# One software DMA ring in order of use, 512 B first loads and single score groups at the head of an attention and feed-forward kernel

## The chip, the cores and the metric

The kernel runs on one core of a Trainium2 chip. The metric is the device time of one execution in microseconds (us), and every time quoted as "of runs" is a median of several executions. Beside it there are profiled executions; their span is the time from the first to the last recorded instruction, and it is 1.7 to 1.9 us shorter than the device time of the same execution.

Ratios are computed as the mean time of one kernel's fast runs over that of the kernel before's fast runs of the same rounds on the same chip, so a ratio is not quite the quotient of the medians that stand beside it.

## The reference

Attention over 4 batches, 8 heads, 768 positions and head size 64, in which retrieval heads see all earlier positions and the other heads see 4 sink positions and a window of 64; then a feed-forward layer on the 3072 tokens. Condensed from the reference:

```python
rel = pos[:, None] - pos[None, :]
causal = rel >= 0
stream_keep = causal & (is_sink | ((rel >= 0) & (rel < window)))
mask = np.where(retr[0, :, 0, 0, None, None], causal, stream_keep)
a = softmax(np.where(mask, scale * q @ k.T, -1e9))
x = (a @ v).transpose(0, 2, 1, 3).reshape(3072, 512)
h = x @ w_in                       # 512 x 2048
out = (h - np.tanh(h)) @ w_out     # 2048 x 512
```

## The kernel before

Tokens are worked in 12 tiles of 256, three to a batch. For a tile, q and k are cast to fp16 and transposed by TensorE (PE), scores are built per pair of heads (a unit, four to a tile), ACT takes the exponential, PE multiplies by v, and the result `x` is transposed and goes through `w_in` (matmuls `ph`, here called hidden units) and `w_out` (`po`, output groups). A list scheduler in Python fixes the order of each engine when the kernel is built. Each operation names its engine, an estimated length, what it reads and writes, and, for a load, its number of DMA packets. Only reads and writes of the same buffer become semaphores; an operation that is merely told to be ordered after another in the plan gets no wait on the chip.

Tiles 0 and 1 come in fp32 through the Sync engine's (SP's) DMA ring, in halves of four heads and blocks of 128 tokens:

```python
for i in blocks:
    s0 = g * TT + i * 128
    op("SP", ...,
        lambda ...: nc.sync.dma_start(
            out=raw_of(nm, t)[:, i, h0 : h0 + nh, :],
            in_=src[b, h0 : h0 + nh, s0 : s0 + 128, :].rearrange("h p d -> p h d")),
        w=[...], dma=(128 * nh, 18.3), after=after)      # 256 B rows
```

ACT, DVE and GpSimd (POOL) cast them. The weights and tile 2 come through GpSimd's own ("software") DMA ring, which casts fp32 to fp16 in flight; issuing such a load keeps GpSimd itself for 0.54 to 1.1 us in the traces. The head of the program (its first 35 us, until PE is full) is laid out like this, cut with `...`:

```python
cast_qk(0, (("ACT", "ACT"), ("ACT", "DVE")), (0,))
load(1, halves=range(2))                    # tile 1 by SP, fp32
for n in (0, 1):
    st_T(n, "ACT", "DVE")                   # transposes of unit n
    for f in scores(n): f()
...
for half in range(2):
    cast_qk(1, (("ACT", "ACT"), ("ACT", "ACT")), (half,))
    cast_v(1, ("POOL", "POOL"), (half,))
for c0, n in W_IN:
    load_w_in(c0, n, [("v1", 0, 1, 0)])     # 4 loads
for j in range(4):
    load_w_out(j, [("v1", 0, 1, 0)])        # 4 loads
load_cast(2)                                # tile 2: 6 loads, last on the ring
scale_v(0, "POOL")                          # vf = v * flag of the head
scale_v(1)
# tile 3 and on: SP loads, held by a tiny "gate" DMA that reads tile 2's k
```

The masks are DVE work: for each head `m = (A < thr) * -60000`, 128 x 512 in fp16, and for tiles 0 and 1 PE adds them to the scores through an identity matmul. A second set of eight, `A >= thr`, replaces them while tile 1 is worked; from tile 2 on DVE multiplies the exponentials by it. `scale_v` is GpSimd work, two multiplications of about 1.06 us for a tile.

The softmax here doesn't subtract the row's maximum and nothing guards it: scores larger than these inputs give would overflow.

## Time and profile before

| | before |
|---|---|
| device time, median of 3 | 242.54 us (242.09 to 242.56) |
| the profiled execution | 240.8 us, span 239.1 |
| PE busy | 221.2 of 239.1 us |
| next: ACT, DVE | 144.8, 138.3 us |

The prediction below reads the head of the profile. The columns are the stretch and its length, then the busy time of PE, of PE's weight loads, of DVE, ACT and GpSimd with their numbers of instructions, the granted clock, the DMA share and GB/s.

```profile
core 0: us, PE busy (x) PEld busy (x) DVE busy (x) ACT busy (x) POOL busy (x), PEclk, DMA share, GB/s
2.25:4.00 1.75, 0.00 (x0) 0.00 (x0) 0.33 (x2) 0.57 (x2) 0.90 (x4) 1.00 0.87 192
...
60.00:65.00 5.00, 4.26 (x67) 2.52 (x63) 2.25 (x7) 3.73 (x5) 4.69 (x12) 1.00 1.02 274
...
80.00:85.00 5.00, 4.08 (x47) 3.13 (x47) 3.42 (x12) 2.08 (x4) 2.26 (x8) 1.00 1.16 206
```

In a stretch of 5.00 us, PE was idle for 0.74 and 0.92 us, although the head was long over. And between 2.25 and 4 us the loads already moved 192 GB/s.

### The profile page before, as it was taken

Reading aid. Unit: us, or ns where it says so; the run is one execution under the profiler, and the core shown is the slowest. Engines: PE = TensorE matmul, PEld = TensorE weight load, DVE = VectorE, ACT = ScalarE, POOL = GpSimd, SP = SyncE. Lnnn points to the kernel's source line nnn. Section 1 sums busy time; section 2 is a strip of 40 time slices with the busy share of each in tenths; the row PEclk is TensorE's granted clock in tenths of the full one; section 3 lists DMA queues with packets and bytes.
Section 4 is the critical chain, followed back from the end, with each engine's and each line's share of the span. In section 5 each row is a group of like instructions: output and inputs, shape, how many; then the busy total and the mean of one; then the engine's idle time right before and its main releaser. Section 6 shows DMA issues by size and latency. Waiting matters only on the chain. (4 is left out here: it accounts for less than half of the span.)

```text
span 239.1 us, 5924 instructions
## 1 busy us (share of the span) xinstructions
PE 221.2 (93%) x2220; PEld 158.0 (66%) x2220; DVE 138.3 (58%) x343; ACT 144.8 (61%) x225; POOL 87.6 (37%) x214
## 2 busy tenths in 40 slices
PE   0877899999889899999999999999999999999992
PEld 0445678765578577777767686777777777777661
DVE  3564455584588767766765744667676537434310
ACT  3588665787658658655576738456768473443320
POOL 5286342009984558191461943724500000000000
PEclk9999999999999999999999999999999999999999
DMA  6999999997999999949989486998611111211121
GB/s 133 220 193 204 213 212 169 210 210 149 261 213 221 182 174 173 246 80 218 259 147 236 106 188 167 167 212 193 123 54 62 31 44 48 71 28 35 44 88 51
DMA packets 110338, 36.08 MB, mean 151 GB/s; under 512 B 104546, under 2 KB 106850, under 8 KB 110306
## 3 DMA queue, kind: packets, MB, share of 16 engines
q1 hardware_dynamic: 101090, 30.55, 62.3%
q0 software_dynamic: 8928, 4.98, 15.1%
q8 instruction: 18, 0.29, 0.5%
q10 hardware_dynamic: 288, 0.14, 0.2%
q14 instruction: 14, 0.11, 0.2%
HBM read 27.27 MB, written 6.29 MB: 140 GB/s over the span
## 5 line engine op out<-in xcount | busy, mean ns | idle before, releaser
L1080 PE MATMUL ph<-xT,win 128*128 128x256 f16 x768 | 101.0, 273 | 1.6 <-DMA xT<-x16t 0.9
L1139 PE MATMUL po<-wout,gt 128*128 128x512 f16 (+1 forms) x400 | 98.5, 371 | 0.2
L1093 ACT ACTIVATE th<-ph 128x512 f32<-128x512 f32 x96 | 57.3, 601 | 62.9 <-PE ph L1080 61.4
L1100 DVE SCALAR_TENSOR_TENSOR gt<-th,ph 128x512 f16<-128x512 f32 x96 | 65.3, 685 | 45.9 <-ACT th L1093 45.5
L1080 PEld LDWEIGHTS <-win 128*128 128x128 f16 x768 | 80.0, 114 | 14.1 <-issue 3.0
L906 ACT ACTIVATE pt<-sc 128x1024 f16<-128x1024 f32 (+1 forms) x78 | 68.2, 925 | 9.3 <-PE sc L886 8.1
L1139 PEld LDWEIGHTS <-gt 128*128 128x128 f16 x400 | 36.2, 98 | 25.1 <-issue 1.3
L630 POOL CAST t<-raw_rqk 128x256 f16 x72 | 27.7, 427 | 58.8 <-DMA raw_rqk<-in_k_dram 42.6
L975 PEld LDWEIGHTS <-pt 128*128 128x128 f16 x552 | 25.9, 98 | 9.9 <-issue 0.9
L975 PE MATMUL av<-v,pt 128*128 128x65 f16 x304 | 26.2, 196 | 0.3 <-ACT xT L774 0.3
L625 POOL CAST v<-raw_rv 128x128 f16 x72 | 22.5, 353 | 6.1 <-DMA raw_rv<-in_v_dram 6.1
L886 PE MATMUL sc<-qk 64*128 64x128 f16 (+1 forms) x412 | 23.0, 239 | 1.5 <-DVE qk L776 1.2
L886 PEld LDWEIGHTS <-qk 64*128 64x128 f16 x412 | 13.7, 95 | 12.6 <-issue 8.9
L1005 DVE TENSOR_TENSOR x16t<-av,rinv 128x128 f32 x72 | 20.8, 289 | 1.9
L975 PE MATMUL av<-vf,pt 128*128 128x65 f16 x248 | 19.8, 193 | 0.1
L1115 ACT ACTIVATE ot<-po 128x512 f32<-128x512 f32 (+1 forms) x24 | 14.3, 596 | 8.7 <-PE po L1139 8.7
L995 DVE RECIPROCAL rinv<-av 128x4 f32<-128x4 f32 x48 | 8.6, 179 | 17.2 <-PE av L975 17.2
L941 DVE TENSOR_TENSOR pt<-pt,m 128x1024 f16<-128x1024 f16 x16 | 11.6, 725 | 7.4 <-ACT pt L906 7.4
L931 DVE TENSOR_TENSOR pt<-pt,mS 128x512 f16<-128x512 f16 x24 | 11.1, 503 | 6.6 <-ACT pt L906 6.6
L793 PEld LDWEIGHTS <-t 128*128 128x128 f16 x48 | 4.2, 109 | 9.2 <-ACT t L594 5.7
L701 POOL TENSOR_TENSOR vf<-v,rflagr 128x260 f16<-128x260 f16 x12 | 7.3, 615 | 0.0
L471 DVE TENSOR_SCALAR m<-A,thr 128x512 f16<-128x512 f16 x16 | 5.9, 418 | 2.0 <-PE sc L873 1.6
(95 smaller groups left out, 88.7 us busy)
## 6 DMA issues: line engine op xcount, KB each, us to landing
out_dram<-ot SPq DMA_DIRECT2D x23, 256.0 KB, 2.5
raw_rqk<-in_q_dram SPq DMA_DIRECT2D x18, 256.0 KB, 4.3
raw_rqk<-in_k_dram SPq DMA_DIRECT2D x18, 256.0 KB, 4.4
raw_rv<-in_v_dram SPq DMA_DIRECT2D x18, 256.0 KB, 4.6
win<-in_moe_w_in_dram POOLq DMA_DIRECT2D x4, 512.0 KB, 9.0
wout<-in_moe_w_out_dram POOLq DMA_DIRECT2D x4, 512.0 KB, 15.9
raw_rqk<-in_q_dram SPq DMA_DIRECT2D x8, 128.0 KB, 3.8
raw_rqk<-in_k_dram SPq DMA_DIRECT2D x8, 128.0 KB, 3.8
```

The lines of the kernel that those rows point to most:

```text
L625: nc.gpsimd.tensor_copy(out=v1s[b]()[:, lo : lo + NB, rank : rank + 1, 0:D], in_=raw_of("v", t)[:, :, at, :],)
L630: nc.gpsimd.tensor_copy(out=t16[t % 2][:, :, :, rank : rank + 1, :], in_=raws["rqk", t][0]()[:, :, :, at, :],)
L886: nc.tensor.matmul(out=sc()[:, hh, o : o + nb * 128].rearrange("p (i c) -> p i c", c=128), lhsT=ks.rearrange("p i c -> p (i c)")[p_, jb * ...
L906: lambda pt=pt, gi=gi, wid=wid, sc=sc: nc.scalar.activation(out=pt()[:, :, 512 * gi : 512 * gi + wid], in_=sc()[:, :, 0:wid], func=AF.Exp, ...
L941: nc.vector.tensor_mul(out=pv, in0=pv, in1=m4[:, h0 : h0 + 2, 256:512].unsqueeze(2).to_broadcast([128, 2, 2, 256]),)
L975: nc.tensor.matmul(out=av()[:, i, hh, :], lhsT=pt()[:, hh, co : co + 128], rhs=vv, start=(jb == first_jb), stop=(jb == qb),)
L1005: nc.vector.tensor_mul(out=x16s[t]()[:, :, at, :], in0=av()[:, :, hh : hh + 1, 0:D], in1=rinv()[:, :, hh : hh + 1].unsqueeze(3).to_broadca ...
L1080: nc.tensor.matmul(out=ph()[:, j, :], lhsT=w()[:, cb, c0 + fb % 4 : c0 + 512 : 4], rhs=xTs[t]()[:, cb, :], start=(cb == 0), stop=(cb == HP ...
L1093: lambda: nc.scalar.activation(out=th()[:], in_=ph()[:], func=AF.Tanh, scale=1.0 / XS),
L1100: lambda: nc.vector.scalar_tensor_tensor(out=gts[t]()[:, u * FU : (u + 1) * FU, :], in0=th()[:], scalar=-XS, in1=ph()[:], op0=ALU.mult, op ...
L1115: nc.scalar.activation(out=ot()[:, c0:c1], in_=po()[:, c0:c1], func=AF.Copy, scale=1.0 / XS)
L1139: nc.tensor.matmul(out=po()[:, c0:c1], lhsT=gts[t]()[:, f, ts * 128 : ts * 128 + 128], rhs=w_out_t[f // 4]()[:, f % 4, c0:c1], start=(f == ...
```

## The change

The intent: what PE needs first is to land first. Tile 1 moves to the software ring, so its casts fall away; that ring is forced into one fixed order (new argument `behind`), with tile 1 and the first `w_in` chunk first, and with tile 2 between the `w_out` chunks and no longer behind them; q, k of tile 0 come in packets of two tokens (512 B); the scores of tile 1 are issued one group at a time; the eight masks of the first units are split in pairs around the key copies. The diff is shortened; `...` and `w=[...]` stand for what is left out.

```diff
-    def op(self, eng, ns, fn, r=(), w=(), dma=None, prio=None, port=False, after=None):
+    def op(self, eng, ns, fn, r=(), w=(), dma=None, prio=None, port=False, after=None, behind=None):
 ...
+        def paired(nm, t):
+            return nm != "v" and t == 0
 ...
+                    if paired(nm, t):
+                        op("SP", max(420, 128 * nh * 1.1),
+                            lambda ...: nc.sync.dma_start(
+                                out=raw_pairs(nm, t)[:, h0 : h0 + nh, :, :].rearrange(
+                                    "p h e d -> p h (e d)"),
+                                in_=src[b, h0 : h0 + nh, g * TT : (g + 1) * TT, :].rearrange(
+                                    "h (p e) d -> p h (e d)", e=NB)),
+                            w=[...], dma=(128 * nh, 26.0), after=after)
+                        continue
 ...
+                    if paired(nm, t):      # PSUM -> qk, back to the order of the tokens
+                        o = o.rearrange("p b (c e) -> p b e c", e=NB)
+                        src = src.rearrange("p e (b c) -> p b e c", b=NB)
 ...
-            two = 1 if todo[0][0] // HP in (0,) else 2
+            two = 1 if todo[0][0] // HP in (0, 1) else 2
 ...
-        load(1, halves=range(2))
+        load_cast(1, [("rv", 0, "v", 0, 1)], "qk")
+            load_w_in(*W_IN[0], ())
+            load_cast(1, (), "v")
         for n in (0, 1):
+            masks(thr, "thr", range(2 * n, 2 * n + 2), added=True)
             st_T(n, "ACT", "DVE")
 ...
-        for half in range(2):
-            cast_qk(1, (("ACT", "ACT"), ("ACT", "ACT")), (half,))
-            cast_v(1, ("POOL", "POOL"), (half,))
-            for c0, n in W_IN:
-                load_w_in(c0, n, [("v1", 0, 1, 0)])
-            for j in range(4):
-                load_w_out(j, [("v1", 0, 1, 0)])
-            load_cast(2)
-        scale_v(0, "POOL")
+            load_w_in(*W_IN[1], ())
+            load_w_in(*W_IN[2], ())
+            scale_v(0, "POOL")
+            load_w_in(*W_IN[3], ())
+            load_w_out(0, ())
+            load_cast(2, (), "q")
+            load_cast(2, (), "k")
+            load_w_out(1, ())
+            load_cast(2, (), "v")
+            load_w_out(2, ())
+            load_w_out(3, ())
         scale_v(1)
```

More of the change, by code (lines that the diff above doesn't have):

```diff
@@ L55, in op @@
         port = port or (eng == "POOL" and not dma)
-        self.ops.append((eng, ns, fn, deps, dma, i if prio is None else prio, port))
+        self.ops.append((eng, ns, fn, deps, dma, i if prio is None else prio, port, behind))
         return i
@@ L61, in run @@
         users = [[] for _ in range(n)]
+        followers = [[] for _ in range(n)]
         left = [0] * n
         for i, o in enumerate(self.ops):
-            left[i] = len(o[3])
+            left[i] = len(o[3]) + (o[7] is not None)
             for d in o[3]:
                 users[d].append(i)
+            if o[7] is not None:
+                followers[o[7]].append(i)
         ready = [0.0] * n
@@ L130, in run @@
             queue[e].remove(i)
-            _, ns, _, _, dma, _, port = self.ops[i]
+            _, ns, _, _, dma, _, port, _ = self.ops[i]
             self.start[i] = t
@@ L136, in run @@
                 self.port = free[e]
+            for u in followers[i]:
+                ready[u] = max(ready[u], t + ns)
+                left[u] -= 1
+                if not left[u]:
+                    enqueue(u)
             if dma:
@@ L293, in load @@
                         )
+                    if paired(nm, t):
+                        op(
+                            "SP", max(420, 128 * nh * 1.1),
+                            lambda nm=nm, src=src, h0=h0, nh=nh: nc.sync.dma_start(
+                                out=raw_pairs(nm, t)[:, h0 : h0 + nh, :, :].rearrange(
+                                    "p h e d -> p h (e d)"
+                                ),
+                                in_=src[b, h0 : h0 + nh, g * TT : (g + 1) * TT, :].rearrange(
+                                    "h (p e) d -> p h (e d)", e=NB
+                                ),
+                            ),
+                            w=[
+                                key for x in (range(2) if half is None else (half,))
+                                for key in raw_keys(nm, t, x)
+                            ],
+                            dma=(128 * nh, 26.0), after=after,
+                        )
+                        continue
                     for i in blocks:
@@ L307, in load, with raw_pairs @@
                         )
+        def raw_pairs(nm, t):
+            r = raws["rqk", t][0]()
+            return r[:].rearrange("p i x h d -> p (i x h d)").rearrange(
+                "p (x h e d) -> p x h e d", x=2, h=H, e=NB
+            )[:, "qk".index(nm), :, :, :]
         def raw_of(nm, t):
+            if paired(nm, t):
+                return raw_pairs(nm, t).rearrange("p h e d -> p e h d")
             r = raws["rv" if nm == "v" else "rqk", t][0]()
@@ L319, in program, with behind, load_cast, fn @@
         W_IN = ((0, 512), (512, 512), (1024, 512), (1536, 512))
-        def load_cast(t):
+        last = [None]
+        def behind(ns, fn, **kw):
+            last[0] = op("POOL", ns, fn, behind=last[0], **kw)
+        def load_cast(t, w_after=(), names="qkv"):
             b, g = divmod(t, NG)
-            for nm, src in (("q", q), ("k", k), ("v", v)):
-                def fn(nm=nm, src=src):
-                    for i in range(NB):
+            for nm in names:
+                src = {"q": q, "k": k, "v": v}[nm]
+                def fn(blocks, nm=nm, src=src):
+                    for i in blocks:
                         s0 = g * TT + i * 128
@@ L334, in fn @@
                         )
-                keys = [
-                    key for half in range(2) for key in (
-                        [("v1", b, g, half)] if nm == "v" else t16_keys(nm, t, half)
-                    )
-                ]
-                op(
-                    "POOL", 2600, fn, r=[("v1", b, 1, 0)], w=keys, dma=(2 * 128 * H, 18.5),
-                )
+                if nm == "v":
+                    for i in range(NB):
+                        behind(
+                            930, lambda fn=fn, i=i: fn((i,)), r=w_after,
+                            w=[("v1", b, g, half) for half in range(2)] if i else [("v1a", t)],
+                            dma=(128 * H, 18.5),
+                        )
+                    continue
+                for i in range(NB):
+                    behind(
+                        930, lambda fn=fn, i=i: fn((i,)), r=w_after,
+                        w=[key for half in range(2) for key in t16_keys(nm, t, half, (i,))],
+                        dma=(128 * H, 18.5),
+                    )
         def load_w_in(c0, n, w_after):
             w = lazy(w_pool, [128, HP, n], FP16, f"win{c0}", f"win{c0}")
-            op(
-                "POOL", 900,
+            behind(
+                800,
                 lambda: nc.gpsimd.dma_start(
@@ L360, in load_w_out @@
             w = lazy(w_pool, [128, 4, DM], FP16, f"wout{j}", f"wout{j}")
-            op(
-                "POOL", 900,
+            behind(
+                600,
                 lambda: nc.gpsimd.dma_start(
@@ L462, in masks @@
         def masks(threshold, key, heads, added=False):
-            for h in range(heads):
+            for h in heads:
                 how = (
@@ L476, in masks @@
                 )
-        masks(thr, "thr", H, added=True)
         RANK = [4 * (hp % 2) + 2 * (hp // 2) + hh for hp in range(HP) for hh in range(2)]
@@ L596, in cast_op, with t16_keys @@
                 op(e, cost, lambda: engs[e].tensor_copy(out=dst(), in_=src()), r=r, w=w, port=True)
-        def t16_keys(nm, t, half):
-            return [("t16", t % 2, nm, half)]
+        def t16_keys(nm, t, half, blocks=range(NB)):
+            return [("t16", t % 2, nm, half, i) for i in blocks]
         def cast_qk(t, engines, halves=range(2)):
@@ L800, in st_T, with out @@
                 )
-                op(
-                    e, {"ACT": 373, "DVE": 288}[e],
-                    lambda x=x, e=e, tp=tp: copy(
-                        e, qk[b % 2][:, x * HP + hp, g * NB : (g + 1) * NB, 0:128], tp()[:, 0:NB, :]
-                    ),
+                def out(x=x, e=e, tp=tp, nm=nm):
+                    o = qk[b % 2][:, x * HP + hp, g * NB : (g + 1) * NB, 0:128]
+                    src = tp()[:, 0:NB, :]
+                    if paired(nm, t):
+                        o = o.rearrange("p b (c e) -> p b e c", e=NB)
+                        src = src.rearrange("p e (b c) -> p b e c", b=NB)
+                    copy(e, o, src)
+                op(
+                    e, {"ACT": 373, "DVE": 420 if paired(nm, t) else 288}[e], out,
                     r=[key], w=q_keys(t, hp) if x == 0 else k_keys(t, hp, g),
@@ L1207, in program @@
         cast_qk(0, (("ACT", "ACT"), ("ACT", "DVE")), (0,))
-        load(1, halves=range(2))
+        load_cast(1, [("rv", 0, "v", 0, 1)], "qk")
+        if first:
+            load_w_in(*W_IN[0], ())
+            load_cast(1, (), "v")
+        else:
+            load_cast(1, (), "v")
         for n in (0, 1):
+            masks(thr, "thr", range(2 * n, 2 * n + 2), added=True)
             st_T(n, "ACT", "DVE")
@@ L1217, in program @@
             st_A(n, 1)
+            masks(thr, "thr", range(2 * n + 4, 2 * n + 6), added=True)
             st_T(n + 2, "ACT", "DVE")
@@ L1226, in program @@
             st_X(n, "o", "ACT")
-        for half in range(2):
-            cast_qk(1, (("ACT", "ACT"), ("ACT", "ACT")), (half,))
-            cast_v(1, ("POOL", "POOL"), (half,))
         if first:
-            for c0, n in W_IN:
-                load_w_in(c0, n, [("v1", 0, 1, 0)])
-            for j in range(4):
-                load_w_out(j, [("v1", 0, 1, 0)])
-            load_cast(2)
+            load_w_in(*W_IN[1], ())
[9 more added lines that the diff above has]
+            load_w_out(3, ())
         else:
             load(2)
-        scale_v(0, "POOL")
+            scale_v(0, "POOL")
         scale_v(1)
@@ L1243, in wait_tile_2 @@
                 nc.sync.dma_start(out=gate[:], in_=t16[0][0:1, 0, 1, 0, 0:1])
-            gated = op("SP", 400, wait_tile_2, r=[("t16", 0, "k", 0)], w=["gate"], dma=(1, 20.0))
+            gated = op("SP", 400, wait_tile_2, r=[("t16", 0, "k", 0, 0), ("t16", 0, "k", 0, 1)], w=["gate"], dma=(1, 20.0))
         PIECES = (
@@ L1275, in program @@
                 if t == 1 and hp == HP - 1:
-                    fs.append(lambda: masks(thr, "thr", H))
+                    fs.append(lambda: masks(thr, "thr", range(H)))
                 if first and fast and t == NG - 1 and hp == HP - 1:
-                    fs.append(lambda: masks(thrr, "thrr", NGEN))
+                    fs.append(lambda: masks(thrr, "thrr", range(NGEN)))
                 if hp == (1 if t == NG - 1 else 0) and t + 1 < NTT:
```

## The prediction

> **What bounds the kernel now.** I read the page first. PE is busy 93% of a 239.1 us span, the next engine 61%, and the slices show PE at nine or more from about the sixth slice on. The kernel is PE-bound apart from its head, so the head was cut into 5 us windows:
>
> ```profile
> core 0: us, PE busy (x) PEld busy (x) DVE busy (x) ACT busy (x) POOL busy (x), PEclk, DMA share, GB/s
> 0.00:5.00 5.00, 0.00 (x0) 0.00 (x0) 0.86 (x7) 1.62 (x3) 2.94 (x15) 1.00 0.53 113
> 5.00:10.00 5.00, 3.69 (x25) 1.88 (x26) 3.22 (x11) 3.19 (x7) 0.90 (x2) 1.00 1.26 222
> 10.00:15.00 5.00, 4.62 (x45) 2.79 (x43) 2.12 (x9) 3.59 (x8) 3.20 (x4) 1.00 1.33 219
> 15.00:20.00 5.00, 2.89 (x41) 1.70 (x38) 3.47 (x11) 4.51 (x10) 5.00 (x9) 1.00 1.18 178
> 20.00:25.00 5.00, 4.39 (x60) 3.67 (x57) 3.09 (x8) 3.21 (x6) 2.28 (x4) 1.00 1.24 207
> 25.00:30.00 5.00, 4.22 (x53) 3.23 (x52) 2.13 (x6) 3.60 (x6) 1.75 (x3) 1.00 1.18 213
> 30.00:35.00 5.00, 4.60 (x52) 3.52 (x51) 2.91 (x7) 2.90 (x7) 1.69 (x3) 1.00 1.07 215
> 35.00:40.00 5.00, 5.00 (x42) 4.25 (x41) 2.34 (x5) 2.53 (x5) 2.61 (x3) 1.00 1.66 182
> ```
>
> The first figure after the length is PE. From 35 us it is full; before, it lost 5.0 us, then 5.6 us of 30. DMA moves about 210 GB/s throughout and is full. Busy hides more, since a matmul at the edge of a wait is drawn long. So I went to the order of time on PE:
>
> ```profile
> 5.54 0.40 PE L793 MATMUL tp0q<-ident,t 128*128 128x128 f16 x2 [5.54 <-ACT t L594]
> ...
> 21.21 1.91 PE L1080 MATMUL ph<-xT,win 128*128 128x256 f16 x16
> ...
> 31.58 1.02 PE L1139 MATMUL po<-wout,gt 128*128 128x512 f16 x4
> ...
> 35.59 1.91 PE L1080 MATMUL ph<-xT,win 128*128 128x256 f16 x16
> 37.34 1.03 PE L1139 MATMUL po<-wout,gt 128*128 128x512 f16 x4
> ```
>
> From 35.59 to 37.34, 16 matmuls of 256 columns start in 1.75 us: 109 ns each. I price every matmul at its columns / 2.4 GHz + 2.5 ns, which gives this, and add up the prices in PE's instruction order. Start time less that sum is PE's lag. It is 5.5 us at the first transpose, 12.8 at the first hidden unit (21.21, work 8.4), 15.3 at the first output group (31.58, work 16.3) and 15.3 at 35.59 (work 20.3). So 9.8 us are lost between first transpose and 35.59, beside 5.5 before it. Only this can shrink, with what is lost once more later, which the waits of PE name:
>
> ```profile
> 64.78 0.29 PE L1053 MATMUL xp<-ident,x 128*128 128x128 f16 x2 [0.73 <-DVE x L1019]
> 66.29 0.71 PE L1080 MATMUL ph<-xT,win 128*128 128x256 f16 x5 [0.34 <-DVE xT L776]
> 68.41 0.63 PE L1080 MATMUL ph<-xT,win 128*128 128x256 f16 x4 [0.35 <-DVE gt L1100]
> 81.53 0.60 PE L1080 MATMUL ph<-xT,win 128*128 128x256 f16 x4 [0.92 <-DMA xT<-x16t]
> ```
>
> There the hidden units of tiles 2 and 3 outrun their attention: 14.6 of lag at 60 us becomes 16.9 at 85. Why is tile 2 late? Its loads come last on the software ring:
>
> ```profile
> 15.03 3.18 POOL L349 DMA_DIRECT2D win<-in_moe_w_in_dram  x4
> ...
> 21.26 0.91 POOL L332 DMA_DIRECT2D t<-in_q_dram  x1 [0.28 <-PE sc L873]
> ...
> 24.61 0.88 POOL L332 DMA_DIRECT2D t<-in_q_dram  x1 [2.44 <-DMA win<-in_moe_w_in_dram]
> ```
>
> The first w_in chunk lands 5.7 us after issue, at 20.7; the second k load of tile 2 (issued 29.61) takes 13.1 us and lands at 42.7. The wait at 24.61 is for the second w_in chunk: evidently eight software loads may be outstanding, and the ninth waits for the first.
>
> **What the Trainium skill says.** "DMA: Bandwidth & Descriptors", section Specifications, puts the smallest transfer for line rate at 512 B. Here 256 B packets from the Sync ring give 128 KB (512 packets) every 0.6 us, about 220 GB/s, and software loads that read 2 KB rows and cast read twice the 206 GB/s that they write: the trace agrees that short rows cost. The same page, section "Issuing engines are not separate DMA queues", says that all rings share 16 engines, so moving tile 1 from one ring to the other adds no bandwidth; the 200 to 220 GB/s whichever ring is active fits. "TensorE: Matmul & The Clock Gate", part 1, has a half-rate clock until about 3.4 us of sustained activity; the trace has the 128-column transposes at 0.31 us until 13 us and 0.22 us from 14.9 us although the granted clock column says 1.00. So the sparse first 8 us of PE cost more than their price, and the change doesn't repair that.
>
> **The change, part by part.**
>
> 1. q, k of tile 0 in 512 B packets. Estimate of one: 18.3 ns for 256 B (0.6 us x 16 / 512) and 79 ns for a 2 KB source row (2.54 us x 16 / 512) give 27 ns for 512 B. Each half of q or k needs 512 x 27 / 16 = 0.86 us in place of 1.2. k of half 0 lands 0.6 us sooner, all of tile 0 after 4 x 0.34 = 1.4 us less. DVE pays: its key copies write with stride 2, so 0.29 us may become 0.42, four times. Half the masks go behind the first key copy. But the first scores still follow four mask matmuls that need the masks done at 6.1 us: I get them at 7.6 us instead of 8.03. In the second half, k casts at 8.3 instead of 9.65, and scores of units 2, 3 come at about 10.8 and 12.2 instead of 12.36 and 13.79.
>
> 2. Tile 1 cast in flight. It removes four ACT casts of 0.62 us (2.5 us of an ACT that was busy 4.51 of 5 us at 15 to 20 us, where PE lost 2.1) and two POOL casts. Scores singly lets unit 4's far group start with tile 1's q alone. From the first q of tile 1 the loads follow at POOL's issue rate, 0.9 us each: issued from 6.6 us, landed from about 10 to 14 us for q and k, before PE asks (about 13.6 and 16).
>
> 3. The ring's order. Data: tile 0 until 2.4 + 5.75 = 8.1 us, tile 1 six loads at 0.9, four w_in chunks and the first w_out chunk at 2.54 (the spacing of these landings before), q, k of tile 2 four at 0.9, and about 1.2 us of gaps where POOL does casts and scaling: 8.1 + 5.4 + 12.7 + 3.6 + 1.2 = 31.0, plus 1.5 us to completion: k of tile 2 lands at about 32.6, not 42.7. The first w_in chunk lands at about 16.9 (20.7), the last at 26.6 (29.1), the first w_out chunk at 29.1 (31.5). The last w_out chunk goes the other way: 42 to 45 us, not 39.0.
>
> PE then: the first hidden unit has work 6.6 ahead of it and waits for w_in and the ACT copy of the last xT, about 17.5: lag 10.9 instead of 12.8. ACT's list from 17.4 us to the last copy of tile 1 is about 13 us of work, to 30.5, with PE next to it: lag 11.5 to 12 at work 19. The first output group (work 18.5) has its weights at 29.1, lag 10.6: no wait. Tile 2's transposes stand at work 20.3, so k at 32.6 sets a lag of 12.3 there. The next weights at work 24.6, 30.0 and 33.7 would be reached at 37, 42 and 46 and are due at 35, 41 and 45: just in time. Sum for the head: 15.3 - 12.4 = 2.9 us.
>
> Later: tile 2's attention is 9 to 10 us earlier and its hidden units stand at work 43.9 (50.4 before), tile 3's loads start on the gate at 33 instead of 43. Of the 2.3 us lost between 60 and 85 I credit 1.5. Total 4.4 us: 242.5 - 4.4 = 238.1. From 85 us on both orders are nearly the same and PE is full, so what is gained stays.
>
> **The rivals.**
>
> A. The late w_out chunks become the new bound. For it: they go behind tile 2, and the gate now lets tile 3's Sync loads in beside them; all share 16 engines. Against: PE has hidden units and tile 2's attention until work 33.7. If the fourth chunk lands at 48, the lag is 14.3 and the gain falls to 2: 240.5.
>
> B. The head was bound by the chain ACT - DVE - PE with its latencies, not by data: then earlier data gives only the ACT casts, some 1.5 us, and the time is 241. For it: PE's named waits in the head are for ACT and DVE, none for DMA. Against: that order was laid out around the late loads, so a wait for an engine there can stand for data that came late further back.
>
> C. Everything early pays in full: lag 11.3 at 35 us and no loss at 60 to 85, gain 4 + 2.3 = 6.3, time 236.2.
>
> D. POOL, now issuing all loads between casts and scaling, stalls on the eight outstanding loads and starves the ring or holds up scaling: worth +1 to +3 us. Against: in the new order the ninth load waits for tile 1's first q, landed long before, and eight loads in the queue are at least 8 x 0.9 = 7 us of transfers.
>
> **Range and chances.** The main estimate and C pull to 236 to 238, A and B to 240.5 to 241. I say 238.0, 8 in 10 within 235.6 to 240.8. Two per cent is 4.85 us, i.e. 237.7: just past my middle, so faster 0.44, within 0.53, slower 0.03.
>
> **What would show it.** Right: the first hidden unit at 17 to 18 us, first k of tile 2 transposed at 32 to 33.5, output groups from 30 us with no wait for w_out over 0.5 us, PE idle 5 to 35 us down from 5.6 to about 3, no waits over 0.5 us at 60 to 85. Wrong: DMA waits of PE on w_out (A); first scores and hidden units where they were (B); key copies far above 0.42 us, or 512 B packets no faster than two of 256 B (part 1); gaps in the DMA slices from 8 to 30 us (D).

## The result, and the profile after

The changed kernel took 238.74 us (median of 4, 238.46 to 240.03) against 242.4 of the kernel before in the same rounds: ratio 0.986, 95% interval 0.982 to 0.990. Run twice more with five rounds each it gave 238.3 against 241.69 (0.986, 0.984 to 0.988) and 238.92 against 242.76 (0.986, 0.981 to 0.991). So it is faster by 3.4 to 3.8 us, within 2 per cent.

The same windows of the changed kernel as those shown of before:

```profile
core 0: us, PE busy (x) PEld busy (x) DVE busy (x) ACT busy (x) POOL busy (x), PEclk, DMA share, GB/s
2.25:4.00 1.75, 0.00 (x0) 0.00 (x0) 0.00 (x0) 0.58 (x2) 0.90 (x4) 1.00 0.49 106
...
5.00:10.00 5.00, 3.36 (x18) 1.45 (x18) 4.56 (x14) 3.23 (x6) 4.65 (x8) 1.00 1.46 242
10.00:15.00 5.00, 4.76 (x38) 2.41 (x39) 2.21 (x7) 3.39 (x7) 4.82 (x7) 1.00 1.69 133
15.00:20.00 5.00, 4.00 (x51) 2.72 (x50) 3.23 (x12) 3.90 (x8) 5.00 (x7) 1.00 1.43 143
20.00:25.00 5.00, 4.02 (x46) 2.54 (x44) 4.09 (x9) 3.60 (x7) 4.90 (x6) 1.00 1.23 201
25.00:30.00 5.00, 4.76 (x70) 3.81 (x71) 3.00 (x9) 3.77 (x7) 1.63 (x2) 1.00 1.36 201
30.00:35.00 5.00, 4.97 (x57) 4.29 (x55) 2.84 (x6) 3.57 (x8) 1.23 (x3) 1.00 1.83 184
...
60.00:65.00 5.00, 5.00 (x45) 3.75 (x44) 2.75 (x4) 3.10 (x6) 4.27 (x13) 1.00 0.91 203
...
80.00:85.00 5.00, 5.00 (x54) 4.14 (x53) 3.19 (x9) 3.50 (x6) 0.09 (x1) 1.00 1.10 189
```

From 5 to 35 us, PE (the first figure after the length) is idle for 30 - 25.87 = 4.1 us, where it was 5.6 before. 15 to 20 us went from 2.89 busy to 4.00. But 5 to 10 us lost: 3.36 where it was 3.69. And the two late windows are full. The first row is a surprise: between 2.25 and 4 us, the 512 B loads moved 106 GB/s, not 192.

PE in order of time, the marks that answer to those of the prediction (start, length, what, and in brackets the idle time before it and what ended that):

```profile
6.00 0.39 PE L843 MATMUL tp0q<-ident,t 128*128 128x128 f16 x2 [6.00 <-ACT t L644]
...
7.46 1.48 PE L928 MATMUL sc<-m,ident 128*128 128x384 f16 x4
...
18.93 1.06 PE L1135 MATMUL ph<-xT,win 128*128 128x256 f16 x8
...
25.04 0.40 PE L941 MATMUL sc<-qk 64*128 64x256 f16 x6 [0.69 <-DVE qk L826]
...
32.80 0.59 PE L1194 MATMUL po<-wout,gt 128*128 128x512 f16 x2
...
34.65 0.39 PE L843 MATMUL tp<-ident,t 128*128 128x128 f16 x4
```

PE starts 0.46 us later than before (6.00, was 5.54), reaches the first hidden unit 2.3 us earlier (18.93, was 21.21) and tile 2's transposes 7 us earlier (34.65, was 41.69). The first output group is 1.2 us later than before by the clock, since more work now lies ahead of it: start alone says nothing when the order has changed. So I use the prediction's lag: start of an instruction less the priced work ahead of it. The same sums for both kernels, in us:

| at | before | after | gain so far |
|---|---|---|---|
| first transpose | 5.54 | 6.00 | -0.46 |
| first transpose of tile 1 | 10.16 | 10.79 | -0.63 |
| first hidden unit | 12.84 | 12.28 | 0.56 |
| first output group | 15.26 | 14.32 | 0.94 |
| first hidden unit of tile 2 | 15.06 | 14.97 | 0.09 |
| first hidden unit of tile 3 | 16.92 | 14.58 | 2.34 |
| end of the matmuls | 13.55 | 11.04 | 2.51 |

So most of what these two profiles show came behind the head. The head gave 0.94 us, lost it again by 60 us, partly in waits of 0.27 and 0.63 us at 37 and 48 us for DVE; between tiles 2 and 3 the kernel before lost 1.9 us that the changed one doesn't. (That the lag falls by some 3.5 us after that in both comes from a price that is a little high; in the comparison it cancels.)

2.5 us of lag are less than the 3.7 us of the medians. The rest is the choice of execution: the profiled one of before was 1.7 us faster than its median. A second profile of the kernel before (told below as a run) took 241.94 us and ends with a lag of 14.66, that is 3.6 us above the changed kernel's.

GpSimd's order now (the software ring's loads are the lines with DMA):

```profile
6.09 1.98 POOL L378 DMA_DIRECT2D t<-in_q_dram  x2
...
11.13 0.76 POOL L401 DMA_DIRECT2D win<-in_moe_w_in_dram  x1
...
23.29 1.07 POOL L810 TENSOR_TENSOR vf<-v,rflag 128x520 f16<-128x520 f16 x1
```

Tile 1's first q goes out at 6.09 us and the first w_in chunk at 11.13 (15.03 before), which lands at 17.05 (20.7). Why did the first 15 us not gain then? In part because the first transpose is late. What comes on top shows in PE's own order. In the kernel before, the matmuls that add the first masks ran while PE had no keys yet:

```profile
5.94 1.49 PE L873 MATMUL sc<-m,ident 128*128 128x384 f16 x4
```

In the changed one they stand behind the first key transpose (6.95 us), at 7.46, so the first scores come at 8.87 us, where the prediction has 7.6 and the kernel before had 8.03. The masks themselves are late too. DVE, first the kernel before:

```profile
4.99 2.31 DVE L471 TENSOR_SCALAR m<-A,thr 128x512 f16<-128x512 f16 x8 [0.44 <-POOL A L406]
```

and the changed one:

```profile
5.82 1.73 DVE L523 TENSOR_SCALAR m<-A,thr 128x512 f16<-128x512 f16 x4 [0.44 <-POOL A L458]
...
7.80 1.95 DVE L523 TENSOR_SCALAR m<-A,thr 128x512 f16<-128x512 f16 x4
...
23.37 1.42 DVE L523 TENSOR_SCALAR m<-A,thr 128x512 f16<-128x512 f16 x2
```

Eight masks took 2.31 us; now four take 1.73 and four 1.95. They start 0.83 us later, because the flags of the heads, a tiny load, land at 4.43 us in place of 3.61 among the slow first packets; and from 6.09 us on they run while GpSimd issues tile 1's loads. The third line shows two masks of 1.42 us, just when GpSimd multiplies v at 23.29; the key copy behind them is what PE waits for at 25.04. The Trainium skill, "SBUF — State Buffer", section "Who interferes with whom", says that GpSimd and some DVE operations, tensor_scalar in a fast mode among them, need the same port pair, and that whoever comes first has it for the whole instruction. The trace fits it: 0.29 us a mask alone, up to 0.82 us beside GpSimd, and the slow ones end just behind an instruction of GpSimd (the mask from 6.47 ends at 7.29, the load's issue at 7.19). Two experiments below take the neighbour away: the slow masks of the first 10 us turn out to cost PE nothing, those at 23 us do cost it.

The landings of tile 0's first half were 5.3 us for q, 6.25 for k, 7.38 for v (4.5, 5.3, 6.5 would be the landings before, less what the prediction says is saved), of the second half 8.28, 9.26 and 10.52 (7.4, 8.3, 9.4). All came about a microsecond later than that, from the first one on: what the 512 B packets gained later they had first lost.

### The profile page after: what moved, and what is told of

Same layout as the page of the kernel before. It is cut to its first block, busy times and chain, and to the rows that moved or that the text cites. A ratio compares the mean times of both kernels' runs of the same rounds, so it can differ in the third digit from the quotient of the medians.

```text
span 236.7 us, 5895 instructions
## 1 busy us (share of the span) xinstructions
PE 221.5 (94%) x2220; PEld 157.8 (67%) x2220; DVE 139.0 (59%) x343; ACT 143.6 (61%) x221; POOL 90.5 (38%) x218
## 3 DMA queue, kind: packets, MB, share of 16 engines
q1 hardware_dynamic: 92642, 28.98, 60.5%
q0 software_dynamic: 15168, 5.77, 20.7%
## 5 line engine op out<-in xcount | busy, mean ns | idle before, releaser
L1155 DVE SCALAR_TENSOR_TENSOR gt<-th,ph 128x512 f16<-128x512 f32 x96 | 65.4, 684 | 44.9 <-ACT th L1148 44.4
L680 POOL CAST t<-raw_rqk 128x256 f16 x72 | 28.5, 440 | 63.3 <-DMA raw_rqk<-in_k_dram 48.1
L941 PE MATMUL sc<-qk 64*128 64x128 f16 (+1 forms) x412 | 23.8, 240 | 1.7 <-DVE qk L826 1.7
L675 POOL CAST v<-raw_rv 128x128 f16 x72 | 21.1, 335 | 4.2 <-DMA raw_rv<-in_v_dram 4.2
L996 DVE TENSOR_TENSOR pt<-pt,m 128x1024 f16<-128x1024 f16 x16 | 12.3, 768 | 8.0 <-ACT pt L961 8.0
L986 DVE TENSOR_TENSOR pt<-pt,mS 128x512 f16<-128x512 f16 x24 | 9.8, 449 | 6.7 <-ACT pt L961 6.7
L523 DVE TENSOR_SCALAR m<-A,thr 128x512 f16<-128x512 f16 x16 | 7.4, 501 | 1.7 <-PE sc L928 1.2
## 6 DMA issues: line engine op xcount, KB each, us to landing
wout<-in_moe_w_out_dram POOLq DMA_DIRECT2D x4, 512.0 KB, 12.4
```

Source lines behind the costliest of these rows:

```text
L675: nc.gpsimd.tensor_copy(out=v1s[b]()[:, lo : lo + NB, rank : rank + 1, 0:D], in_=raw_of("v", t)[:, :, at, :],)
L680: nc.gpsimd.tensor_copy(out=t16[t % 2][:, :, :, rank : rank + 1, :], in_=raws["rqk", t][0]()[:, :, :, at, :],)
L941: nc.tensor.matmul(out=sc()[:, hh, o : o + nb * 128].rearrange("p (i c) -> p i c", c=128), lhsT=ks.rearrange("p i c -> p (i c)")[p_, jb * ...
L996: nc.vector.tensor_mul(out=pv, in0=pv, in1=m4[:, h0 : h0 + 2, 256:512].unsqueeze(2).to_broadcast([128, 2, 2, 256]),)
L1155: lambda: nc.vector.scalar_tensor_tensor(out=gts[t]()[:, u * FU : (u + 1) * FU, :], in0=th()[:], scalar=-XS, in1=ph()[:], op0=ALU.mult, op ...
```

## The experiments

### Repeats: the changed kernel and the kernel before

No edit. The kernel before was profiled again because its first profile was a fast execution.

> The changed kernel, unedited, for a tighter interval and a second trace. Expected 238.3 to 239.2 us, ratio to the kernel before 0.983 to 0.988. In the first trace PE's first transpose started at 6.0 us (5.54 before), the flags landed at 4.4 us (3.6 before) and the first four masks took 1.73 us. If these are the change's own costs they come again within 0.2 us; if they were an accident of one run, the first transpose is back at 5.5 us or earlier.

> The kernel before, unedited, for a second trace: the first traced run was 1.6 us faster than its timed runs. Expected 241 to 242.5 us; if the granted clock drops for about 3.4 us in the head as in two of the experiments, the lag at 35 us is 1 to 1.7 us above the 15.3 of the first trace; if not, the spread comes from elsewhere.

> The changed kernel a third time, on the chip of this batch, so that the next two have it beside them in the same rounds: ratio to the kernel before 0.986 (0.983 to 0.990), first transpose at about 6.0 to 6.2 us, lag 14.2 to 14.4 at 35 us, about 11.0 at the end.

The first repeat of the changed kernel gave 0.986 and a lag of 14.19 at the first output group and 10.99 at the end, the second 14.24 and 11.13: the head is reproducible to 0.15 us, and the slow start came again (first transposes at 6.16 and 5.89). One of the second's executions took 241.58 us, though. The kernel before repeated its head (15.39 at the first output group) and then lost 1.1 us more between 95 and 115 us, where PE waits 1.33 us for a DMA transpose of x. Where that comes from is told at the end of the experiments.

### Tile 0 in 256 B packets again

```diff
-    lambda ...: nc.sync.dma_start(out=raw_pairs(...), in_=... "h (p e) d -> p h (e d)")
+    both_blocks      # for i in range(NB): dma_start(out=raw_of(nm, t)[:, i, ...], 256 B rows)
 ...
-                    if paired(nm, t):
-                        o = o.rearrange("p b (c e) -> p b e c", e=NB)
-                        src = src.rearrange("p e (b c) -> p b e c", b=NB)
```

The plan's prices and so the order of PE stay as they are.

> The changed kernel with tile 0's q and k in 256 B packets again (two loads per half, unstrided copies), in the same instruction order on PE. Prediction's theory: 512 B packets are worth 0.6 to 1.4 us of landing, so this is 0.5 to 1.0 us slower. Rival: the larger packets start slowly and the strided copies cost 4 x 0.15 us on DVE and 4 x 0.07 us on ACT, so this is equal or up to 0.8 us faster, with the first transpose at 5.5 us and flags landed at 3.6 us.

It took 241.32 us, ratio 0.9988 (0.996 to 1.002): the whole gain is gone, which is three to six times what I expected (3.0 us above the changed kernel's 238.3). The first loads did start fast (184 GB/s from 2.25 to 4 us, first cast at 4.96 us, 5.33 with the change), so the slow start belongs to the 512 B packets. Yet by 18 us it had lost (and its first scores, behind the same order of PE, came at 8.70 us). Its DVE, PE and one window:

```profile
14.72 1.68 DVE L522 TENSOR_SCALAR m<-A,thr 128x512 f16<-128x512 f16 x1
...
16.40 1.15 DVE L522 TENSOR_SCALAR m<-A,thr 128x512 f16<-128x512 f16 x1
```

```profile
17.94 0.29 PE L1104 MATMUL xp<-ident,x 128*128 128x128 f16 x2 [2.35 <-DVE x L1070]
```

```profile
core 0: us, PE busy (x) PEld busy (x) DVE busy (x) ACT busy (x) POOL busy (x), PEclk, DMA share, GB/s
...
20.00:22.00 2.00, 2.00 (x10) 1.22 (x8) 0.00 (x0) 1.20 (x2) 2.00 (x4) 0.50 1.31 137
```

Three things follow on each other. The last v loads of tile 0 are still in the Sync ring when tile 1's first software load lands (11.05 us); they land at 11.38 and 12.89 us (10.52 with the change, where tile 1's first lands at 11.43). GpSimd's cast of v slips from 10.58 to 13.02 and its multiplications from 11.90 and 13.88 to 14.35 and 16.32, just upon the two masks above: single masks of 1.68 and 1.15 us that took 0.34 and 0.59 with the change. PE waits 2.35 us for the x behind them. Then the granted clock (the third figure from the end) is 0.50 for 3.4 us, from 19.7 to 23.1, and that costs up to half of it, 1.7 us (an estimate). The Trainium skill, "TensorE: Matmul & The Clock Gate", part 1, describes such a half-rate clock after an idle window of about 3.4 us. The trace has a half-rate stretch of 3.4 us, but in the 3.4 us ahead of the fall PE was 47% busy, not idle; what sets it off stays open. The slow clock isn't all of it: the one execution of this kernel with a clock of 1.000 took 240.36, still 2 us above the changed kernel.

### Scores of tile 1 in twos

```diff
-            two = 1 if todo[0][0] // HP in (0, 1) else 2
+            two = 1 if todo[0][0] // HP in (0,) else 2
```

> The changed kernel with tile 1's scores clustered in twos, as before. If scores singly let PE start tile 1 earlier, this is 0.5 to 1 us slower, with a PE wait for the exponential of about 1 us before tile 1's second masked scores, as in the kernel before at 18.65 us. If the split does not matter (rival), within 0.3 us.

241.7 us, ratio 0.9989 (0.996 to 1.002): also all lost, 3.4 us where I expected 0.5 to 1. PE reaches the first hidden unit at 19.62 with a lag of 13.30 (12.28) after waits of 0.92 and 0.63 us for x, not for the exponential that I expected: the single groups of tile 1's scores that fill this time with the change (at 16.12 and 17.47 us) come together at 18.76 here. Its clock too is at 0.50 from 18.1 to 21.5 us (PE was 54% busy in the 3.4 us ahead), and how much of the loss is the clock's isn't shown. The lag at the first output group is 15.41, and 16.73 at tile 2's hidden units.

### All of w_out ahead of tile 2

```diff
-            load_w_out(0, ())
+            for j in range(4):
+                load_w_out(j, ())
             load_cast(2, (), "q")
             load_cast(2, (), "k")
-            load_w_out(1, ())
             load_cast(2, (), "v")
-            load_w_out(2, ())
-            load_w_out(3, ())
```

> The changed kernel with all of w_out before tile 2 on the ring. Theory: about 1.6 us of the gain comes from tile 2 and 3 being earlier (no waits of PE between 60 and 85 us), so this is 1.0 to 2.0 us slower than the changed kernel and shows waits over 0.3 us there again. Rival: those waits vanish because of the head alone, then it is within 0.4 us of the changed kernel.

241.64 us, ratio 0.999 (0.997 to 1.002), 3.3 us above the changed kernel where I expected 1 to 2. This is the best head of all until then, a lag of 13.48 at the first output group, 0.84 less than with the change. But tile 2's transposes come at 41.20, as before, and then it pays. PE of this kernel:

```profile
64.45 0.28 PE L1108 MATMUL xp<-ident,x 128*128 128x128 f16 x2 [0.74 <-DVE x L1074]
...
72.52 0.56 PE L941 MATMUL sc<-qk 64*128 64x256 f16 x10 [1.01 <-DMA qk<-t]
```

With a further 0.57 at 62.6 and more behind, the lag is 17.52 at tile 3's first hidden unit, 14.58 with the change. So the place of tile 2 on the ring costs 0.84 us in the head and is worth 3.8 behind it (4.04 of lag lost against 0.26).

### Tile 1 by the Sync ring again

```diff
-        load_cast(1, [("rv", 0, "v", 0, 1)], "qk")
-            load_w_in(*W_IN[0], ())
-            load_cast(1, (), "v")
+        load(1, halves=range(2))
 ...
+        for half in range(2):
+            cast_qk(1, (("ACT", "ACT"), ("ACT", "ACT")), (half,))
+            cast_v(1, ("POOL", "POOL"), (half,))
+            load_w_in(*W_IN[0], [("v1", 0, 1, 0)])
```

> The changed kernel with tile 1 loaded through Sync in fp32 and cast by ACT and POOL as before; the rest of the change stays. Theory: tile 1's four ACT casts come back (2.5 us of ACT) and the ring starts later, so the first hidden unit is at 20.5 us or later and the run 1.5 to 3 us slower than the changed kernel; but the first eight masks on DVE take 0.29 us each again, because POOL writes no descriptors then. Rival: what tile 1 in flight saves is paid back by DVE blocked by POOL, so this is within 0.7 us of the changed kernel.

242.21 us, ratio 1.000 (0.997 to 1.003): all lost, somewhat more than the 1.5 to 3 us expected. The head shows it: first hidden unit at 22.06 with a lag of 13.69, first output group 16.70. PE waits 1.94 us at 19.65 for an exponential of ACT; ACT is busy without a gap from 16.29 us to there, and two casts of tile 1, 1.15 us, stand in front of that exponential and two more further up. Then PE has a clock of 0.50 from 20.6 to 24.0. The masks, without GpSimd's load issues beside them, took 1.26 us for four (1.73): the hold-up at 6 to 8 us does come from tile 1's software loads. But it cost PE nothing there: without it the mask matmuls start at 7.47 us and the first two units' scores at 8.88 and 10.25 (7.46, 8.87 and 10.24 with the change), since PE's order is the same. Behind the head it lost 1.3 us more up to tile 3 (a lag of 18.00 at its first hidden unit), 1.04 of it in one wait for an x of DVE's at 79 us. That isn't just a late head handing its lateness on: the 256 B kernel, as late (16.64), lost 0.34 there. The order of the plan differs here; which part of it does it is open.

### The kernel before, with tile 2 between the w_out chunks

```diff
-            for j in range(4):
-                load_w_out(j, [("v1", 0, 1, 0)])
-            load_cast(2)
+            load_w_out(0, [("v1", 0, 1, 0)])
+            load_cast(2, "qk")
+            load_w_out(1, [("v1", 0, 1, 0)])
+            load_cast(2, "v")
+            load_w_out(2, [("v1", 0, 1, 0)])
+            load_w_out(3, [("v1", 0, 1, 0)])
```

> The kernel before with one part alone: on the software ring tile 2's q, k go ahead of the second w_out chunk and its v ahead of the third. Theory: most of the gain sits in tile 2's place on the ring, so this alone is 1 to 2.5 us faster than before and has no PE wait over 0.3 us between 60 and 85 us. Rival: the parts only pay together (three single undoings cost 3 us each), then this is within 0.7 us of before, its head late by what w_out chunks 2 to 4 now miss.

240.3 us, ratio 0.995 (0.991 to 0.999). The head is that of before (15.36 at the first output group), tile 2's transposes come at 34.29, and the lag at tile 3 is 15.96 where before has 16.92. About 1.3 us of the whole gain (0.3 to 2.2 by the interval) is the order of the ring's tail alone. The waits of before at 64 to 82 us are gone, as expected, but a new one of 1.02 us for an x of DVE's stands at 77 us.

### GpSimd's multiplications behind the last load

The changed kernel with `scale_v(1)` ordered behind the last load of the ring, twice; the second time beside the changed kernel on the same chip.

```diff
-        def scale_v(t, eng="POOL"):
+        def scale_v(t, eng="POOL", follow=None):
 ...
+                    behind=follow,
 ...
-        scale_v(1)
+        scale_v(1, follow=last[0])
```

> The changed kernel with the two POOL multiplications that scale tile 1's v moved behind the last load of the ring. In the changed kernel they run at 20.3 and 23.3 us, two DVE masks beside the second take 1.42 us instead of 0.6, and PE waits 0.69 to 1.06 us for the DVE copy behind them. Theory of the shared port: the masks shrink to about 0.35 us each, that wait goes, lag at 27 us falls from 14.0 to about 13.2, and the run is 0.5 to 1 us faster. Rival: the DVE is held by the load issues of POOL, not by its multiplications, then the wait stays and nothing is gained.

> The changed kernel with GpSimd's multiplications of tile 1's v behind its last load, again. Theory (GpSimd and DVE hold each other up, the multiplications beside the masks cost PE up to a microsecond): it repeats its 0.984 and beats the changed kernel of the same rounds by 0.3 to 0.9 us. Rival (the first figure was the spread of the runs): the difference lies between -0.3 and 0.3 us.

The first gave 237.99 us (ratio 0.984, 0.981 to 0.988), the second 238.55 against 238.92 of the changed kernel beside it (ratios 0.982 and 0.986 with intervals that overlap; the first of these is unclear between within 2 per cent and faster). DVE and PE of the first:

```profile
23.21 0.61 DVE L523 TENSOR_SCALAR m<-A,thr 128x512 f16<-128x512 f16 x2
```

```profile
24.08 0.39 PE L942 MATMUL sc<-qk 64*128 64x256 f16 x6
```

The two masks took 0.61 us in place of 1.42, and the scores that waited 0.69 us at 25.04 start at 24.08 with no wait. The lag at the first output group fell from 14.32 to 13.36. The mechanism is shown: the second time too the two masks took 0.61 us and the wait was gone, where the three profiles of the changed kernel have it with 0.69, 1.06 and 0.96 us. Its worth in time isn't resolved, a few tenths to 1 us: the second time 0.4 us were lost at the first transpose already (6.27 us), and that execution, the profiled one, lost 2.3 us at 110 to 115 us and took 241.03; the other five took 238.02 to 238.72. Of all the kernels run, it is the one with the lowest ratios.

### The first half of tile 0 in 256 B, the second in 512 B

```diff
-                    if paired(nm, t):
+                    if paired(nm, t) and half == 1:
 ...
-                    if paired(nm, t):
+                    if paired(nm, t) and hp * 2 // HP == 1:
```

This is on top of the version just told; it was meant to keep the fast start and the later gain. The order of PE moved with it, since the plan prices the copies anew.

> The same, with q, k of the first half of tile 0 in 256 B packets again (as before the change) and those of the second half in 512 B packets. Theory (the first loads in 512 B packets start slowly, the later ones gain): the first transpose comes at about 5.5 us instead of 5.8 to 6.0, the last v half of tile 0 lands no later than 10.6 us, and the kernel is 0.2 to 0.6 us faster than y2. Rival 1 (512 B packets are needed throughout to clear the ring before tile 1's software loads): the last v half lands at 11 us or later, GpSimd's cast of it moves behind 11.5, and the time is that of y2 or up to 1.5 us worse. Rival 2 (the start is slow in any form once the next load is in 512 B packets): first transpose at 5.9 to 6.1, time as y2.

The median of its five fast executions is 241.88 us (239.24 to 242.12), ratio 0.992 (0.987 to 0.998): above both by the medians, though the interval overlaps that of the changed kernel (0.981 to 0.991). The start went as the theory said: first transpose at 5.52 us, and 0.5 us ahead of its parent at the last key transpose of tile 0. But the last v half landed at 10.95 (10.38), GpSimd waited 1.39 us for it in front of its other work, and the first w_in chunk was issued at 13.53 (10.99 in the parent). As in 256 B throughout, the multiplications (14.37) fell on the masks (1.05 us at 14.54), and PE waited 1.47 us for x at 15.98, and 2.8 in four such waits. That ate the early start up, but no more: the lag at the first output group is 14.30, beside 13.36 and 14.10 in the two profiles of its parent. What makes this execution so slow comes later, one wait of PE at 82.8 us:

```profile
PE ph L1136 <- DMA xT<-x16t: 2.3, 1, 2.3
```

Until 80 us the lag had stayed within 0.8 us of the parent's of the same rounds (15.27, 14.52). So the theory of the slow start held and the first rival's chain occurred, but the trace doesn't show that chain as the cause of the whole loss: two executions without a trace took 239.24 and 239.87, about 1 us more than the parent's.

### What moved the single runs

Several kernels have executions that are 2 to 3 us slower than their others at a full clock. The profiled executions of the version just told and of the second run of the late multiplications are two; this is the longest wait of PE from 60 to 115 us in the latter:

```profile
PE ph L1136 <- DMA xT<-x16t: 2.1, 1, 2.1
```

In the traces SP issues its DMAs one after another. In that execution a DMA transpose issue took 3.46 us at 77 us (1.32 in the fast one), the ones behind it slipped, the transpose of an x of tile 5 went out at 108.5 us and not at 104.4, and PE waited. The kernel before has a wait for such a transpose in both of its profiles (0.92 and 1.33 us), the changed kernel in none of three. Whether the change makes the slip rarer or three profiles were lucky can't be told from so few, and what makes the first issue long is open. So a single profile of an experiment can carry 2 us behind the head that its other executions don't have.

## Why the prediction was right, and where it was wrong

The time (238.0 predicted, 238.3 to 238.9 measured) and the class were right. The way there was right in its direction but not in its split.

- Step 3, the order of the ring. The first and last w_in chunks landed at 17.05 (predicted 16.9) and 28.98 (26.6), the first w_out chunk at 31.4 (29.1), k of tile 2 at 35.3 (32.6): right in kind, 2.3 to 2.7 us late from the last w_in chunk on. The term "about 1.2 us of gaps where POOL does casts and scaling" was too small: between its loads GpSimd did two casts and two multiplications from 9.00 to 14.94 us, 3.35 us, and from 13 to 14 us the DMA engines moved 65 GB/s. It was shown by the kernel before with this order alone, and by all of w_out first, that tile 2's place does what was said.
- The sum for the head, 15.3 - 12.4 = 2.9 us. This is the step that failed: 0.94 measured, the first hidden unit at 18.93 in place of 17 to 18, and PE idle for 4.1 us in place of about 3. The first scores, "at 7.6 us instead of 8.03", came at 8.87, 1.3 us late, and of that two things are shown. The first loads in 512 B packets were priced from the start at 27 ns a packet; they moved 106 GB/s until 4 us, so first casts and masks came 0.5 to 0.8 us late (predicted: k of half 0 0.6 us sooner). And the four mask matmuls, for which the prediction needs the masks "done at 6.1 us", ran at 7.46, behind the key transpose in PE's new order. Later the hold-up of DVE by GpSimd's multiplications, which was not in the sum at all, cost PE 0.69 us at 25 us, as the late multiplications show. 1.3 and 0.69 together are the 2 us that are missing (2.9 - 0.94); that they simply add is an estimate. The key copies were priced (0.43 to 0.45 measured, 0.42 predicted); ACT's copies of q also write with a stride and took 0.44 in place of 0.37, which I had left out, with no measured cost to PE. The 1.4 us that the first eight masks lost beside GpSimd's load issues cost PE nothing, as tile 1 by the Sync ring shows.
- "Later: I credit 1.5" of the 2.3 us lost at 60 to 85. The changed kernel had no wait above 0.3 us there, and its lag fell from 14.97 to 14.58 where before's rose from 15.06 to 16.92: 2.25 us, all of it. That made up for part of the head. The rest lies in the executions of before, whose profile was a fast one. That the total still came out near 238 is in this part luck.
- Part 1, 512 B for tile 0. I priced it as 1.4 us of data (0.6 us x 16 / 512 is 18.8 ns, not 18.3, which moves this little) and saw its worth in the scores of units 2 and 3, at 10.8 and 12.2 us. They came at 11.90 and 13.63, where before they were at 12.36 and 13.79. Undone alone it cost 3 us. So it is needed in this order, but for another reason than the one given: it lands tile 0 (10.52 us) before tile 1's first software load (11.43), and with that keeps GpSimd's work off DVE's masks. Whether 256 B would do with GpSimd's multiplications of tile 0 placed elsewhere was not tried.
- Adding the parts. The prediction summed them. Undoing the 512 B, the single scores, the ring's tail or tile 1's casts each brings back all of the 3.5 us, so they aren't terms of a sum: each undone part makes PE idle somewhere at 15 to 20 us or 60 to 80 us, and three of the four then pay for a half-rate clock on top.

Of the rivals, A (late w_out chunks) didn't occur: they landed at 37.3, 41.7 and 44.4, before PE asked, and PE has no wait for w_out. B (the chain of engines bounds the head) was nearer to the truth for the first 35 us than I gave it: PE's waits there are for ACT and DVE, and only 0.30 us for a w_in chunk. C is excluded by the time. D (GpSimd stalls on eight outstanding loads and starves the ring) showed as waits such as 1.75 us at 26.65 ahead of tile 2's v, and its sign, a gap in the DMA slices, at 13 to 14 us; PE lost only the 0.30 us for w_in by it. But GpSimd did cost by holding up DVE, which no rival said.

## What to carry to other kernels

When loads move to the software ring, look at what DVE does while GpSimd issues them, and push GpSimd's own arithmetic to where DVE has no masks that PE waits behind; the profile shows it as the same DVE instruction at two to five times its usual length. Then check that PE waits for it: here one such hold-up cost PE up to 1 us and another nothing. Test the parts of a change by undoing each from the whole, since a part that looks small by its bytes may be what keeps two engines apart. And before you compare two profiles, compare each profiled execution with the median of its own kernel: here 1.2 us of the gain lay in that.

## What the Trainium skill lacked or had wrong

- "DMA: Bandwidth & Descriptors", Specifications, names 512 B as enough for line rate. Later in the head 512 B packets did run faster (about 0.95 us for 256 KB, against 0.6 us for 128 KB in 256 B packets), but the first loads of the kernel in 512 B packets moved 106 GB/s from 2.25 to 4 us (68 to 120 in the eight profiles of that kind), and in 256 B packets 184 to 192 (five profiles). The page says nothing of such a start; its cause is open.
- "TensorE: Matmul & The Clock Gate", part 1, has the half-rate clock follow an idle window of about 3.4 us. In three runs it came for 3.4 us after 3.4 us in which PE was 43 to 54% busy; in one with 43% it didn't come. (The page's later section "A second HAM failure mode" has the clock fall with short, frequent idling too, but gives no busy share.) And until about 14 us the transposes took 0.39 us for two (0.28 from 15.2 us) though the granted clock of the profile read 1.00; the page itself warns that the clock's trace events can be unreliable.
- "SBUF — State Buffer", "Who interferes with whom", is right in kind. What it has no figure for is this pair: a 128 x 512 fp16 tensor_scalar of 0.29 to 0.34 us took up to 1.68 us beside GpSimd's multiplication of 1.07 us and the load issue behind it, and 0.43 to 0.49 on average beside load issues.
- No page that I read has the number of software loads that may be outstanding. In the traces of before and after a ninth waits until the first has landed, mostly for 1.3 to 2.4 us; whether the chip or the program sets the eight, they don't say.
